# One DRAIN instruction on GpSimd behind the row scatters of the fourth expert tile

## The chip, the core and the metric

The kernel runs on one core of a Trainium2 chip. The core has five engines with queues of their own: TensorE (PE, whose weight loads are shown as PEld), VectorE (DVE), ScalarE (ACT), GpSimd (POOL) and SyncE (SP, which here mostly issues transfers). The metric is the device time of one execution in microseconds; the number compared is the median over several runs.

## What is computed

Three stages follow one another: a chunked state-space scan over 4 x 8 heads, a two-layer network with a leaky ReLU, and a layer of eight experts in which each of the 3072 rows goes through the one expert that its gate picks. The last stage in the reference:

```python
e_idx = np.argmax(logits, axis=1)
gate_w = probs[np.arange(N), e_idx]
out = np.zeros((N, D), dtype=np.float32)
for e in range(E):
    mask = e_idx == e
    h = np.maximum(x[mask] @ w1[e], 0.0)
    out[mask] = gate_w[mask, None] * (h @ w2[e])
```

with N = 3072, D = 256, E = 8 and 1024 hidden columns.

## The kernel before

The scan, the network and the routing are worked off in 128-row chunks and 512-row blocks. For the expert stage the kernel builds, on the chip, a list of row numbers for each expert, and then works through six expert tiles of 512 rows; a seventh and more follow under a condition, which on these inputs is not met.

Three kinds of steps use GpSimd's indirect transfers, in which GpSimd itself makes the descriptors from a list of indices:

- `put` writes 128 row numbers at a time into the experts' lists (L835, tile `il`): 24 transfers.
- `ga` fetches the rows of an expert tile, four transfers of 128 rows each (L977, tile `xg`): 24 for six tiles.
- `sc` scatters 128 finished rows into the output (L1086, `out_dram`): four for each tile, 24 in all.

`oe` on ScalarE (L1082) scales 128 result rows by their gate weight into a buffer, and the `sc` of the same numbers waits for it. `sc.3.3` is the last scatter of the fourth tile (tiles count from 0), `sc.4.0` the first of the fifth.

The order of the instructions on every engine is written out by hand: the string `PLAN` is split into words, each word calls a step, and an engine works its instructions in the order in which the steps wrote them.

```python
for token in PLAN.split():
    fn, *args = token.split(".")
    ...
        STEPS[fn](*args)

u = nc.values_load(tabu, min_val=0, max_val=NFIN, skip_runtime_bounds_check_because=WHY)
```

Behind the last word each engine loads `u`, the number of further tiles (L1197), and branches over their code (L1202). There GpSimd has a few waits and one instruction that the trace calls INC_SWDGE_SEM. What is shown under L1251, the line that opens the program's context, is the end of the program, which the framework adds: every engine has a DRAIN, SP waits for the semaphores of the others, and all meet twice at GpSimd before the program is over. L1238 is its beginning, with a DRAIN on every engine too.

Of the kernel before, what the change touches and what calls it, by code (L numbers as in the profile page):

```python
# [112 lines left out]
    re.3.5 rl.3.5 sl2.4.1 m1.3.6 m2.3.3 re.3.6 rl.3.6 sc.2.1 m1.3.7 sc.2.2 m1.4.0 sh1.5.0 sc.2.3 sh1.5.1 sl1.5.0  # L113
    m2.3.4 re.3.7 sl1.5.1 m2.3.5 re.4.0 rl.3.7 xt.5 rl.4.0 m1.4.1 xe.5.1 xe.5.0 xf.5.1 m2.3.6 re.4.1 xf.5.0 rl.4.1
    m1.4.2 m2.3.7 re.4.2 rl.4.2 m1.4.3 sh2.5.1 sh2.5.0 sl2.5.1 m1.4.4 re.4.3 m2.4.0 oe.3.1 rl.4.3 oe.3.0 oe.3.3
    sl2.5.0 sc.3.0 m1.4.5 oe.3.2 re.4.4 sc.3.1 rl.4.4 m2.4.1 sc.3.2 m2.4.2 re.4.5 rl.4.5 sc.3.3 m1.4.6 m2.4.3 re.4.6
    rl.4.6 m1.4.7 m1.5.0 re.4.7 rl.4.7 m2.4.4 re.5.0 rl.5.0 m1.5.1 m1.5.2 re.5.1 rl.5.1 m2.4.5 re.5.2 rl.5.2 m1.5.3
    m1.5.4 re.5.3 rl.5.3 m2.4.6 re.5.4 rl.5.4 m1.5.5 m1.5.6 re.5.5 rl.5.5 re.5.6 m1.5.7 rl.5.6 m2.4.7 re.5.7 rl.5.7
    oe.4.1 m2q.5.0 oe.4.2 oe.4.0 oe.4.3 sc.4.0 sc.4.1 m2q.5.1 oe.5.0 sc.4.2 sc.4.3 m2q.5.2 oe.5.1 sc.5.0 sc.5.1
# [5 lines left out]
def kernel(  # L125
# [53 lines left out]
    v, s, g, t_ = nc.vector, nc.scalar, nc.gpsimd, nc.tensor  # L179
# [780 lines left out]
    def e_ix(i):  # L960
        tab, k = tl[i]
        vi = nc.values_load(tab[:, 1, k:k + 1], engines=[ENG.SP], min_val=0, max_val=NE * NT - T, skip_runtime_bounds_check_because=WHY)
        gi = sp.tile([P, NQ], I32, tag="gi", name="gi", bufs=6)
        r = nc.sync.dma_start(out=gi, in_=il[bass.ds(vi, T), :].rearrange("(q p) o -> p (q o)", p=P))
        for w in puts:
            tc.add_manual_dep(
                r.ins, w.name, mybir.DependencyInfo(mybir.DependencyClass.Sync, mybir.DependencyReason.DATA),
                reason="the list read here",
            )
        ex.setdefault(i, {})["gi"] = gi  # L970
# [22 lines left out]
    def e_sh(i, t, k):  # L993
        r, hi, lo = e_raw(i, t, k)
        s.copy(out=hi, in_=r)

    def e_sl(i, t, k):
        r, hi, lo = e_raw(i, t, k)
        (g if t == 2 and k == 1 else v).tensor_tensor(out=lo, in0=r, in1=hi.bitcast(F32), op=ALU.subtract)
# [159 lines left out]
    def exp(c, q):  # L1159
# [17 lines left out]
        "tf1": lambda: te.update(fi=table_final()) or next(te["fi"]), "tf2": lambda: next(te["fi"]), "tf3": lambda: next(te["fi"]),  # L1177
        "tf4": lambda: next(te["fi"], None),
        "w1": e_w1, "ixs": lambda: [e_ix(i) for i in range(EARLY, EARLY + NSTAT)], "w2": e_w2, "ix": e_ix, "ga": e_ga, "xt": e_xt, "xe": e_xe, "xf": e_xf, "m1": e_m1, "re": e_re, "rl": e_rl,
        "m2": e_m2, "m2q": e_m2q, "oe": e_oe, "sc": e_sc,  # L1180
        "sh1": lambda i, k: e_sh(i, 1, k), "sl1": lambda i, k: e_sl(i, 1, k),
        "sh2": lambda i, k: e_sh(i, 2, k), "sl2": lambda i, k: e_sl(i, 2, k),
    }
# [72 lines left out]
```

## Time and profile before

| | |
|---|---|
| median of 3 runs | 523.72 us (523.45 to 525.17) |
| the profiled execution's own time | 520.77 us |
| its span, first to last instruction | 519.1 us |
| busy: PE / DVE / ACT / POOL | 494.6 / 328.2 / 288.4 / 137.9 us |
| indirect transfers issued by GpSimd | 72 |
| start of the last one | 507.20 us |

The span is what the trace covers; 1.7 us of the profiled execution's own time lie around it. Busy time of an engine holds no register, branch, semaphore or DRAIN instructions; those stand under the name of the engine's queue, as POOLq or SPq. Times within the span count from its start.

### The profile page before, as it was taken

Reading aid. Unit: us, or ns where it says so; the run is one execution under the profiler, and the core shown is the slowest. Engines: PE = TensorE matmul, PEld = TensorE weight load, DVE = VectorE, ACT = ScalarE, POOL = GpSimd, SP = SyncE. Lnnn points to the kernel's source line nnn. Section 1 sums busy time; section 2 is a strip of 40 time slices with the busy share of each in tenths; the row PEclk is TensorE's granted clock in tenths of the full one; section 3 lists DMA queues with packets and bytes.
Section 4 is the critical chain, followed back from the end, with each engine's and each line's share of the span. In section 5 each row is a group of like instructions: output and inputs, shape, how many; then the busy total and the mean of one; then the engine's idle time right before and its main releaser. Section 6 shows DMA issues by size and latency. Waiting matters only on the chain.

```text
span 519.1 us, 8927 instructions
## 1 busy us (share of the span) xinstructions
PE 494.6 (95%) x3263; PEld 393.6 (76%) x3266; DVE 328.2 (63%) x719; ACT 288.4 (56%) x626; POOL 137.9 (27%) x137
## 2 busy tenths in 40 slices
PE   7879899999999999999999999999999999999990
PEld 4536677787777777777877788888899999899890
DVE  5897999887668664866478777555744544343300
ACT  5858899675475656556564474455525554454220
POOL 5342323040204010121002072300225643715050
PEclk8999999999999999999999999999999999999996
DMA  7988943385713641337000850400018844201010
GB/s 187 171 201 204 277 90 68 62 90 26 161 12 63 113 101 11 61 51 166 0 1 2 259 176 17 40 5 0 2 43 251 289 149 159 70 24 40 1 68 20
DMA packets 120150, 48.41 MB, mean 93 GB/s; under 512 B 84065, under 2 KB 113890, under 8 KB 120098
## 3 DMA queue, kind: packets, MB, share of 16 engines
q1 hardware_dynamic: 117026, 41.35, 36.4%
q0 software_dynamic: 3072, 6.41, 3.8%
q8 instruction: 28, 0.46, 0.5%
q14 instruction: 24, 0.20, 0.2%
HBM read 41.14 MB, written 6.60 MB: 92 GB/s over the span
## 4 chain that ended last, share of the span: by engine, by line
PE 78%; issue 8%; DVE 4%; POOL 3%; ACT 3%; DMA 1%; POOLq 0%; ACTq 0%; DVEq 0%; SPq 0%
PE y L695 24%; PE h L655 24%; PE hp L1025 9%; PE o L1056 9%; PE cb L512 2%; PE psy L552 2%; POOL out_dram L1086 2%; PE psy L547 1%; PE xps L1006 1%; PE yr L852 1%; DMA e<-cumd 1%; DVE hb L605 1%; DVE hb L606 1%; PE lp L734 1%; DVE gg L667 1%
## 5 line engine op out<-in xcount | busy, mean ns | idle before, releaser
L662 ACT ACTIVATE sa<-h 128x512 f32<-128x512 f32 x96 | 56.8, 596 | 72.5 <-PE h L655 71.4
L667 DVE TENSOR_TENSOR gg<-sa,h 128x512 f32<-128x512 f32 x96 | 65.4, 685 | 49.1 <-ACT sa L662 48.9
L677 DVE TENSOR_TENSOR gl<-gg,gh 128x512 fp32r<-128x512 f32 x96 | 71.2, 748 | 14.9 <-ACT gh L672 14.0
L655 PE MATMUL h<-xh,wih 128*128 128x512 f32 x192 | 78.4, 409 | 1.0 <-DVE gg L667 1.0
L695 PE MATMUL y<-gh,woh 128*128 128x512 f32 x192 | 79.2, 412 | 0.0
L695 PE MATMUL y<-gl,woh 128*128 128x512 f32 x192 | 75.4, 393 | 1.4 <-DVE gl L677 1.4
L655 PE MATMUL h<-xl,wih 128*128 128x512 f32 x192 | 75.1, 391 | 0.9 <-DVE xl L576 0.9
L695 PE MATMUL y<-gh,wol 128*128 128x512 f32 x192 | 75.1, 391 | 0.0
L655 PE MATMUL h<-xh,wil 128*128 128x512 f32 x192 | 75.0, 391 | 0.0
L672 ACT CAST gh<-gg 128x512 fp32r<-128x512 f32 x96 | 59.1, 619 | 25.6 <-DVE gg L667 21.2
L1043 DVE SCALAR_TENSOR_TENSOR hl<-hp,hh 128x512 fp32r<-128x512 f32 x48 | 32.9, 689 | 59.5 <-ACT hh L1039 59.2
L1056 PE MATMUL o<-w2s,hh 128*128 128x256 f32 x384 | 70.0, 282 | 0.0
L1025 PE MATMUL hp<-x2h,w1s 128*128 128x512 f32 x192 | 65.5, 394 | 0.1
L1056 PEld LDWEIGHTS o<-w2s,hh 128*128 128x128 f32 x384 | 61.2, 190 | 2.2
L1039 ACT ACTIVATE hh<-hp 128x512 fp32r<-128x512 f32 x48 | 28.6, 598 | 60.8 <-PE hp L1025 58.5
L1056 PE MATMUL o<-w2s,hl 128*128 128x256 f32 x192 | 54.1, 282 | 0.0
L835 POOL DMA_INDIRECT il<-ids,pi x24 | 24.8, 1035 | 105.4 <-DVE base L826 68.2
L417 ACT ACTIVATE e<-e,ncum 128x128 f32<-128x128 f32 x160 | 50.5, 394 | 0.0
L399 POOL TENSOR_SCALAR_AFFINE_SELECT e<-e 128x1024 f32<-128x1024 f32 x20 | 24.2, 1211 | 90.9 <-DMA e<-cumd 84.9
L655 PEld LDWEIGHTS h<-xh,wih 128*128 128x128 f32 x192 | 36.0, 188 | 12.7 <-DVE gg L667 2.9
L695 PEld LDWEIGHTS y<-gh,woh 128*128 128x128 f32 x192 | 36.1, 188 | 11.8 <-issue 4.7
L695 PEld LDWEIGHTS y<-gl,woh 128*128 128x128 f32 x192 | 36.1, 188 | 8.4 <-DVE gl L677 2.3
(209 smaller groups left out, 807.8 us busy)
## 6 DMA issues: line engine op xcount, KB each, us to landing
r<-in_moe_w_dram SPq DMA_DIRECT2D x24, 512.0 KB, 5.3
e<-cumd SPq DMA_DIRECT2D x20, 512.0 KB, 5.2
raw<-in_moe_w_in_dram SPq DMA_DIRECT2D x4, 1024.0 KB, 6.2
raw<-in_moe_w_out_dram SPq DMA_DIRECT2D x4, 1024.0 KB, 6.7
yx<-ysb SPq DMA_DIRECT2D x6, 528.0 KB, 7.4
xt<-in_x_dram SPq DMA_DIRECT2D x24, 128.0 KB, 4.5
ct<-in_C_dram SPq DMA_DIRECT2D x24, 64.0 KB, 4.9
bt<-in_B_dram SPq DMA_DIRECT2D x24, 64.0 KB, 4.2
```

The lines of the kernel that those rows point to most:

```text
L417: s.activation(out=e[:, h, :], in_=i, func=AF.Exp, bias=ncum[:, cc, b * H + h:b * H + h + 1])
L655: t_.matmul(h, lhsT=w[:, k, fs], rhs=xx[:, k, :], start=(i == 0), stop=(i == 5))
L662: s.activation(out=d["sa"], in_=d["h"], func=AF.Copy, scale=0.01)
L667: v.tensor_tensor(out=d["gg"], in0=d["sa"], in1=d["h"], op=ALU.max)
L672: s.copy(out=d["gh"], in_=d["gg"])
L677: v.tensor_tensor(out=gl, in0=d["gg"], in1=d["gh"].bitcast(F32), op=ALU.subtract)
L695: t_.matmul(y_t[j][k], lhsT=w[:, f, ds], rhs=gg, start=(f == 0 and i == 0), stop=(f == NF - 1 and i == 2))
L835: w = g.indirect_dma_start(out=il[:], out_offset=IndirectOffsetOnAxis(ap=pi[:, q:q + 1], axis=0), in_=ids[:, c0 + q:c0 + q + 1], in_offset ...
L1025: t_.matmul(d["hp", f], lhsT=d[1][:, k, part, fs], rhs=xx[:, k, :], start=(n == 0), stop=(n == 5))
L1039: s.activation(out=e_h(i, f, "hh"), in_=ex[i]["hp", f], func=AF.Relu)
L1043: v.scalar_tensor_tensor(out=e_h(i, f, "hl"), in0=d["hp", f], scalar=0.0, in1=d["hh", f].bitcast(F32), op0=ALU.max, op1=ALU.subtract)
L1056: t_.matmul(d["o", q], lhsT=d[h, f][:, q * P:(q + 1) * P], rhs=d[2][:, f, part, :], start=(start and n == 0), stop=(f == NF2 - 1 and n == ...
```

## The change

A word `dr` is added to `PLAN` right behind `sc.3.3`, and the table of steps gets an entry for it that writes a GpSimd DRAIN. Nothing else is added, taken away or moved.

```diff
-    sl2.5.0 sc.3.0 m1.4.5 oe.3.2 re.4.4 sc.3.1 rl.4.4 m2.4.1 sc.3.2 m2.4.2 re.4.5 rl.4.5 sc.3.3 m1.4.6 m2.4.3 re.4.6
+    sl2.5.0 sc.3.0 m1.4.5 oe.3.2 re.4.4 sc.3.1 rl.4.4 m2.4.1 sc.3.2 m2.4.2 re.4.5 rl.4.5 sc.3.3 dr m1.4.6 m2.4.3 re.4.6
...
-        "m2": e_m2, "m2q": e_m2q, "oe": e_oe, "sc": e_sc,
+        "dr": lambda: g.drain(), "m2": e_m2, "m2q": e_m2q, "oe": e_oe, "sc": e_sc,
```

The rows below are GpSimd's order around this place, the change against the kernel before, from the third scatter of the fourth tile to the load of `u`; a name such as `o_5699` is the buffer that the scatter writes out. Register moves, waits and DRAINs are not among the rows of this view.

```order
 L1086 DMA out_dram<-o_5712,gi 3072x256
 L1086 DMA out_dram<-o_5699,gi 3072x256
-L1086 DMA out_dram<-o_5940,gi 3072x256
-L1086 DMA out_dram<-o_5911,gi 3072x256
-L1086 DMA out_dram<-o_5938,gi 3072x256
-L1086 DMA out_dram<-o_5942,gi 3072x256
+L1086 DMA out_dram<-o_5941,gi 3072x256
+L1086 DMA out_dram<-o_5912,gi 3072x256
+L1086 DMA out_dram<-o_5939,gi 3072x256
+L1086 DMA out_dram<-o_5943,gi 3072x256
```

Nothing has moved: from here on the buffers' numbers are one higher, because the DRAIN took a number. It stands between `o_5699` (`sc.3.3`) and `o_5941` (`sc.4.0`), and carries no wait on a semaphore and no post to one. The other engines keep their order.

## Rows read from the trace of the kernel before

**Rows 1.** The page: span, and busy time of each engine.
```profile
span 519.1 us, 8927 instructions
PE 494.6 (95%) x3263; PEld 393.6 (76%) x3266; DVE 328.2 (63%) x719; ACT 288.4 (56%) x626; POOL 137.9 (27%) x137
```
**Rows 2.** Busy time in stretches of the end: us, engines, PE clock, DMA share, GB/s.
```profile
475.00:496.00 21.00, 20.95 (x125) 18.34 (x124) 6.92 (x10) 7.25 (x14) 0.00 (x0) 1.00 0.02 7
...
508.20:509.40 1.20, 0.00 (x0) 0.00 (x0) 0.00 (x0) 0.00 (x0) 0.00 (x0) 1.00 0.33 116
...
512.30:518.20 5.90, 0.00 (x0) 0.00 (x0) 0.00 (x0) 0.00 (x0) 0.00 (x0) 0.50 0.00 0
```
**Rows 3.** Timeline of POOL at the end: start, us, instruction, idle time before it.
```profile
473.92 0.98 POOL L1086 DMA_INDIRECT out_dram<-o,gi  x1 [0.30 <-issue]
496.32 0.98 POOL L1086 DMA_INDIRECT out_dram<-o,gi  x1 [21.41 <-ACT o L1082]
497.60 0.98 POOL L1086 DMA_INDIRECT out_dram<-o,gi  x1 [0.30 <-issue]
...
507.20 0.98 POOL L1086 DMA_INDIRECT out_dram<-o,gi  x1 [1.87 <-ACT o L1082]
```
**Rows 4.** Line 1202, behind the branch: count, ns min/median/max, first and last start.
```profile
L1202 POOLq EVENT_SEMAPHORE  x5: 17/43/43, 510.2 to 510.5; - x5
...
L1202 POOLq INC_SWDGE_SEM  x1: 1628/1628/1628, 510.6 to 510.6; - x1
```
**Rows 5.** Line 1251, the program's end, from 510 to 518.3 us, POOL alone.
```profile
L1251 POOLq DRAIN  x1: 5945/5945/5945, 512.3 to 512.3; - x1
L1251 POOLq EVENT_SEMAPHORE  x1: 17/17/17, 518.3 to 518.3; - x1
```
**Rows 6.** The same line from 512 to 513.5 us, SP alone.
```profile
L1251 SPq EVENT_SEMAPHORE  x12: 27/28/28, 512.2 to 512.9; - x12
L1251 SPq DRAIN  x2: 7/10/13, 512.9 to 513.0; - x2
```
**Rows 7.** Waits of SP's queue, 500 to 521 us: us in total, times, longest.
```profile
SPq L1251 <- DMA out_dram<-o,gi: 68.3, 1, 68.3
SPq L1251 <- PEq L1251: 6.0, 2, 5.4
```
**Rows 8.** Line 1251 from 518.3 us on, POOL alone.
```profile
L1251 POOLq EVENT_SEMAPHORE  x3: 17/17/17, 518.3 to 518.9; - x3
L1251 POOLq DRAIN  x2: 40/74/107, 518.4 to 518.8; - x2
```
**Rows 9.** Line 1238, the program's beginning, POOL alone.
```profile
L1238 POOLq INC_SWDGE_SEM  x1: 27/27/27, 0.2 to 0.2; - x1
...
L1238 POOLq DRAIN  x1: 188/188/188, 0.4 to 0.4; - x1
```
**Rows 10.** DMA issues: count, median us from issue to landing.
```profile
il<-ids,pi POOLq DMA_INDIRECT x24, 9.0
xg<-yx,gi POOLq DMA_INDIRECT x24, 4.1
out_dram<-o,gi POOLq DMA_INDIRECT x24, 2.5
```
**Rows 11.** The last twelve scatters, from 465 us on: durations and landing.
```profile
L1086 POOL DMA_INDIRECT out_dram<-o,gi x12: 977/979/1801, 469.3 to 507.2; - x12
...
DMA to landing us min/median/max: 2.4/2.4/3.2
```
**Rows 12.** The first indirect transfers, line 835, the whole span.
```profile
L835 POOL DMA_INDIRECT il<-ids,pi x24: 975/978/1401, 109.6 to 380.1; - x24
```

## The prediction

> **What bounds the kernel now.** I begin with the page. TensorE is busy for 494.6 of 519.1 us [rows 1], so over most of the span only less work for TensorE would shorten the kernel. The change adds one instruction on GpSimd, which is busy for 137.9 us, so the question is narrow: is GpSimd waited for anywhere near the DRAIN, and does the DRAIN alter anything later?
>
> The busy time in stretches answers the first half. From 475 to 496 us GpSimd does nothing at all, while TensorE is busy for 20.95 of 21 us [rows 2]. The timeline of GpSimd shows the same from its side: `sc.3.3` starts at 473.92 and takes 0.98, so it ends at 474.90, and `sc.4.0` starts at 496.32 because ScalarE's `o` was not there earlier, after 21.41 us of idle time [rows 3]. The DRAIN goes into this gap.
>
> The second half needs the end of the program, where TensorE is done and every microsecond counts fully. The last scatter ends at 507.20 + 0.98 = 508.18 us [rows 3], yet the span lasts to 519.1 [rows 1]: a tail of 10.9 us. I take it apart by the lines behind the branch. GpSimd's waits there start at 510.2, and INC_SWDGE_SEM runs from 510.6 for 1.63 us [rows 4]. Then comes GpSimd's DRAIN at the end of the program: from 512.3, for 5.945 us, up to 518.2 [rows 5]. Behind it 0.84 us of meeting and clearing are left. In the stretch from 512.3 to 518.2 no engine does anything and the DMA share is 0.00 [rows 2]. So more than half of the tail is one DRAIN, alone on the chip, and everybody waits for it: SP is through its own end at 513.0 [rows 6] and then waits 5.4 us, which the view puts down to PE [rows 7], though PE is idle all that time [rows 2].
>
> What does this DRAIN do for 5.9 us? It isn't waiting for work that the profile shows: GpSimd's last instruction ended at 508.18, and the last scatter, issued at 507.20, landed 2.4 to 3.2 us later [rows 3, 11], before the DRAIN began; its data moves from 508.2 to 509.4, with a DMA share of 0.33 [rows 2]. Nor is a DRAIN on GpSimd slow in itself. The same trace has three more: 0.188 us at the beginning of the program, behind nothing but five small instructions [rows 9], and 0.107 and 0.040 us right behind the long one [rows 8]. What sets the long one apart is what lies between it and the previous DRAIN: the whole program, with 24 + 24 + 24 = 72 indirect transfers [rows 10]. Its neighbour tells the same story. INC_SWDGE_SEM took 0.027 us at the beginning [rows 9] and 1.628 us behind the 72 [rows 4]. My reading is that GpSimd keeps something for each indirect transfer it has issued, that nothing cleans it up on the way, and that the DRAIN goes through this list one by one.
>
> **The change part by part.** There is one part, with one cost and one effect.
>
> The cost of the new DRAIN. 64 of the 72 indirect transfers stand ahead of it (24 `put`, 24 `ga`, 16 `sc` of four tiles), 8 behind it (`sc.4.0` to `sc.5.3`). If the long DRAIN is a base of about 0.1 us [rows 8] and a share for each transfer, the share is (5.945 - 0.1) / 72 = 0.081 us. The new DRAIN then takes 0.1 + 64 x 0.081 = 5.3 us. It may first wait for `sc.3.3` to land, at the latest 3.2 us behind its issue [rows 11], at 477.1. So it is over by 482.4. The only thing queued behind it is `sc.4.0`, which ScalarE releases at 496.3; the cover is 21.4 us, 14 us of it to spare. While it lasts nobody waits for GpSimd: the buffers that ScalarE needs back are freed by the landing of the scatters, not by the DRAIN. Without the cover the 5.3 us would delay the eight scatters one for one. I cost it at nothing.
>
> The effect on the last DRAIN. With 8 transfers behind it, it takes 0.1 + 8 x 0.081 = 0.75 us instead of 5.945, 5.2 less.
>
> The effect on INC_SWDGE_SEM is bounded from both sides. At most nothing changes: 1.63 us [rows 4]. At least, if it grows in a straight line from 0.027, it is 0.027 + 8 / 72 x 1.60 = 0.20 us. I take 0.5: it also releases SP (SP's first step of the end passes at 512.2, just as it finishes [rows 6, 4]), so I leave it eight posts at the 0.043 us of a semaphore step [rows 4], 0.34, and scale the other 1.29 by 8 / 72, 0.14. It gains 1.1 us.
>
> What is late next is SP. Its end runs from 512.2 to 513.0 [rows 6], 0.8 us behind INC_SWDGE_SEM. With the old 1.63 us, GpSimd's DRAIN would end at 512.27 + 0.75 = 513.02 and SP arrives at 513.0: a tie, and GpSimd's next step, at 518.26 before [rows 5], comes at 513.07. That is 5.2 us earlier. With 0.5 us both move up by 1.1: 6.3 us earlier. With 0.2 us, 6.6 earlier. So SP doesn't take back what the DRAIN gives, since it hangs on the same INC_SWDGE_SEM.
>
> The sum: 520.77 - 6.3 = **514.5 us** for the profiled execution. The runs shown have a median of 523.72, 2.95 us above that execution. The tail is the same program in both, so I take the 6.3 off the median: **517.4 us**, 1.2% less.
>
> A rule of the Trainium skill speaks against this. PSUM — Partial Sum Buffer, Engine vs sequencer instructions, says that a drain waits for the engine to go fully idle. Read strictly, a DRAIN on an idle engine is short, one written ahead of it changes nothing, and the time would stay at 523.7. This case's trace doesn't agree: the engine's last instruction and the last landing lie ahead of the 5.945 us [rows 3, 5, 11].
>
> **The rivals.** *A fixed toll.* The long DRAIN costs 5.9 us whenever any indirect transfer came before it, be it 8 or 72: fetching a routine, say, or setting up the descriptors anew. Then the new DRAIN takes about 6 us in the gap, the last one 5.9 us again, and the time stays at 523.7. For it: all three short DRAINs have no indirect transfer between them and the DRAIN ahead, so no row tells "some" from "many". Against it: INC_SWDGE_SEM grew as well, and a step of 1.6 us next to one of 5.9 fits a list that both go through better than one routine that is fetched. GPSIMD Engine Reference, in Instruction dispatch, gives about 6 us for the first call into freshly loaded code, with no instruction of its own in the profile; no run here shows yet whether that is what the DRAIN pays.
>
> *A short list.* GpSimd keeps only the last so many transfers. With 16 of them the share is 5.85 / 16 = 0.37 us, and the last DRAIN still takes 0.1 + 8 x 0.37 = 3.0 us, 2.9 less: 520.8. Against it: the transfers' durations show no cleaning up on the way, with 0.98 us at the median from the first to the last [rows 11, 12].
>
> *A slow restart, slower than before.* The DRAIN throws away what GpSimd had prepared, and `sc.4.0` pays to get it back, while the last DRAIN stays at 5.9 us. If the restart costs as much as the long DRAIN, `sc.4.0` ends 6 us late, at 503.3, and the other seven follow at 0.98 + 0.30 = 1.28 us [rows 3]: 503.3 + 9.0 = 512.3 instead of 508.18, so 527.8. The point from which it decides: the last two scatters have some 1.9 us of slack between them, so a restart below 1.9 us is swallowed, and one above shows. Against it: the very first indirect transfer took 1.40 us, only 0.42 more than the median [rows 12].
>
> That the DRAIN isn't where it says is no rival: the order has it between `sc.3.3` and `sc.4.0`. A DRAIN that outlasts the gap would need 21.4 us, four times what the long one took with more behind it.
>
> **How the numbers follow.** Likeliest, 0.82: the list, 517.4, with 517.1 to 518.5 from the bounds on INC_SWDGE_SEM. The short list 0.05, 520.8. The fixed toll 0.09, 523.7. The slow restart 0.04, 527.8. The runs of before spread over 1.7 us, and the profiled execution lies 3 us below their median, so a new median can lie a microsecond or two off the old one; I widen the first case to 515.5 to 520.0, which alone holds about 8 in 10. About 0.3% (1.6 us) is what a measurement of this kernel can tell from no change. Faster takes in the list and the short list, less a little for the spread: 0.86. Same: the toll, 0.09. Slower: 0.05.
>
> **What the profile of the changed kernel would show.** A POOLq DRAIN at about 475 us, of 5 to 8 us; 5 to 6 means no waiting for the landing. `sc.4.0` at 496.3 as before, with its 0.98 us. INC_SWDGE_SEM of 0.2 to 0.6 us; 1.6 would put the gain at 5.2. The last POOLq DRAIN of 0.6 to 0.9 us. SP's end beginning at about 511.1, and a span of 512.5 to 513.9. I am wrong if the last DRAIN is still near 5.9 us (a toll), near 3 (a short list), or if the scatters of the fifth tile begin late.

## The result and the profile after

The changed kernel takes 517.9 us at the median of 4 runs (515.77 to 518.36), the kernel before 524.18 us at the median of 4 runs on the same chip (523.45 to 525.17). The ratio is 0.9871, with a 95% interval of 0.9838 to 0.9904; of 524.18 us that is 5.0 to 8.5 us less. The forecast was 6.3 us less, 517.4 us. The profiled execution took 515.77 us, where 514.5 was forecast.

The page of the changed kernel gives its span and its busy times. The span is 5.0 us shorter, and the busy times are within 1.2 us of those before [rows 1]:

```profile
span 514.1 us, 8931 instructions
PE 495.4 (96%) x3266; PEld 393.5 (77%) x3266; DVE 327.0 (64%) x719; ACT 288.1 (56%) x626; POOL 138.1 (27%) x137
```

The group of the new line, 1180, in the changed kernel: one DRAIN, with its duration in ns and its start in us.

```profile
L1180 POOLq DRAIN  x1: 9710/9710/9710, 471.3 to 471.3; - x1
```

The timeline of POOL in the changed kernel, around that DRAIN and at the end:

```profile
474.75 0.98 POOL L1086 DMA_INDIRECT out_dram<-o,gi  x1 [0.30 <-issue]
497.13 0.98 POOL L1086 DMA_INDIRECT out_dram<-o,gi  x1 [21.41 <-ACT o L1082]
...
508.02 0.98 POOL L1086 DMA_INDIRECT out_dram<-o,gi  x1 [0.48 <-ACT o L1082]
```

The two are read together. The DRAIN's record begins at 471.3, while scatters of the fourth tile are still running, so its 9.71 us hold their time too. What the DRAIN costs is read from its end: 471.3 + 9.71 = 481.0 us. `sc.3.3` ends at 474.75 + 0.98 = 475.73, so the DRAIN holds GpSimd for 5.3 us behind it. `sc.4.0` starts at 497.13, 16 us after the DRAIN is over, and what released it is ScalarE's `o`, after the same 21.41 us of idle time as before [rows 3]. The cover held, and nothing came late because of the DRAIN. In the stretch of the gap TensorE is busy for 21.95 of 22 us, at the full granted clock as before [rows 2]:

```profile
475.00:497.00 22.00, 21.95 (x130) 19.16 (x129) 6.92 (x10) 7.43 (x14) 0.72 (x1) 1.00 0.04 13
```

Now the end. Line 1202 of the changed kernel, behind the branch (count, ns, first and last start), answers to [rows 4]:

```profile
L1202 POOLq EVENT_SEMAPHORE  x5: 17/43/43, 511.7 to 512.0; - x5
L1202 POOLq INC_SWDGE_SEM  x1: 348/348/348, 512.1 to 512.1; - x1
```

Line 1251, the program's end, from 511 to 513.3 us, POOL alone, answers to [rows 5]:

```profile
L1251 POOLq DRAIN  x1: 707/707/707, 512.5 to 512.5; - x1
L1251 POOLq EVENT_SEMAPHORE  x1: 17/17/17, 513.3 to 513.3; - x1
```

The same line from 511 to 513.3 us, SP alone, answers to [rows 6]:

```profile
L1251 SPq EVENT_SEMAPHORE  x12: 27/28/28, 512.4 to 513.1; - x12
L1251 SPq DRAIN  x2: 7/10/13, 513.2 to 513.2; - x2
```

And the waits of SP's queue from 500 us on answer to [rows 7]:

```profile
SPq L1251 <- PEq L1251: 0.7, 2, 0.5
```

The last DRAIN took 0.707 us instead of 5.945, INC_SWDGE_SEM 0.348 instead of 1.628. SP's 6.0 us of waiting for the others became 0.7. GpSimd's DRAIN is over at 512.5 + 0.7 = 513.2, the time at which SP comes through its own steps. So the two tie, and neither gives anything back.

The tail from the end of the last scatter to the end of the span is 514.1 - (508.02 + 0.98) = 5.1 us, against 10.9 us before: 5.8 less in this pair of executions. In experiment e8, a second execution of the same kernel, it is 4.4.

### The profile page after: what moved, and what is told of

Its sections match the earlier page's. It is cut to its first block, busy times and chain, and to the rows that moved or that the text cites. A ratio compares the mean times of both kernels' runs of the same rounds, so it can differ in the third digit from the quotient of the medians.

```text
span 514.1 us, 8931 instructions
## 1 busy us (share of the span) xinstructions
PE 495.4 (96%) x3266; PEld 393.5 (77%) x3266; DVE 327.0 (64%) x719; ACT 288.1 (56%) x626; POOL 138.1 (27%) x137
## 4 chain that ended last, share of the span: by engine, by line
PE 72%; issue 8%; ACT 6%; DVE 5%; POOL 2%; DMA 2%; SPq 2%; POOLq 1%; ACTq 0%; DVEq 0%
PE y L695 22%; PE h L655 22%; PE hp L1025 10%; PE o L1056 9%; PE cb L512 2%; PE psy L552 2%; POOL out_dram L1086 1%; SPq L392 1%; DVE hb L606 1%; PE psy L547 1%; DMA ct<-in_C_dram 1%; PE xps L1006 1%; PE yr L852 1%; DMA e<-cumd 1%; DVE hb L605 1%
## 5 line engine op out<-in xcount | busy, mean ns | idle before, releaser
L1025 PEld LDWEIGHTS hp<-x2h,w1s 128*128 128x128 f32 x192 | 36.1, 188 | 8.3 <-issue 0.9
```

Source lines behind the costliest of these rows:

```text
L1025: t_.matmul(d["hp", f], lhsT=d[1][:, k, part, fs], rhs=xx[:, k, :], start=(n == 0), stop=(n == 5))
```

## The experiments

The theory: GpSimd keeps something for each indirect transfer, a DRAIN goes through what has gathered since the DRAIN ahead of it, and so does INC_SWDGE_SEM. The rivals from before the result, the fixed toll, the short list and the slow restart, had already lost with the 0.707 us. Three were left that can give the same 0.707 us: that the DRAIN goes by the time since the one before it, that it goes by the count of all of GpSimd's instructions, or that the cost hangs on the bytes or rows moved. A further question was where a DRAIN may stand, and whether the gain can be had without the gap. Each kernel is timed against the kernel before on its own chip. In all but e3, e9 and e10 the computation is that of the kernel before, and the word `dr` has the same entry in the table as in the change.

**e1, behind the first tile's scatters.** 44 transfers ahead of the DRAIN, 28 behind.

```diff
-    ... w1.4 m2.1.5 sl1.3.1 xe.2.1 xe.2.0 sc.0.3
+    ... w1.4 m2.1.5 sl1.3.1 xe.2.1 xe.2.0 sc.0.3 dr
```

> The one DRAIN stands behind sc.0.3, in an idle stretch of 10.4 us: 44 indirect transfers ahead of it, 28 behind. The list theory (a base and a share for each transfer since the last DRAIN; from 5.945 us with 72 and 0.707 with 8 the share is 0.082 and the base 0.05): last DRAIN 2.34 us, INC_SWDGE_SEM 0.75 (0.020 for each transfer, 0.19 base), the new DRAIN over 3.7 us after sc.0.3 ends, the time 4.5 us below the kernel before, a ratio of 0.991. Rival, time since the last DRAIN (the same two points give 0.011 us for each us): last DRAIN 1.4 us, time 5.5 us or more below. Rival, all GpSimd instructions since the last DRAIN (140 and 9, now 32): last DRAIN 1.65 us.

519.84 against 524.93 us, ratio 0.9919 (0.9894 to 0.9945). Line 1251 of e1 at the end, POOL alone; the longest of its three DRAINs is the one in question:

```profile
L1251 POOLq DRAIN  x3: 46/107/2341, 514.1 to 517.0; - x3
```

Line 1202 of e1, POOL alone:

```profile
L1202 POOLq INC_SWDGE_SEM  x1: 748/748/748, 513.4 to 513.4; - x1
```

28 transfers behind give 2.341 us and 0.748 us, between the values at 8 and at 72 and on a straight line with them. The rivals of time and of all instructions put other values there and fall, and so does any list with a limit of 28 or less.

One expectation missed. The new DRAIN ends at 419.6, 5.8 us behind `sc.0.3` (412.83 + 1.00 = 413.83), where the share for 44 transfers gives 3.7. The stretch covered it, but the size is off by 2.1 us; what the traces show of it stands beside e6.

**e2, ahead of the first indirect transfer.** None ahead, all 72 behind.

```diff
-    r3.0 yr.0.0 be.0 y.17 yc.0.0 mask.11 gl.18 put.0 yr.0.1
+    r3.0 yr.0.0 be.0 y.17 yc.0.0 mask.11 gl.18 dr put.0 yr.0.1
```

> The one DRAIN stands ahead of the first put: no indirect transfer ahead of it, 72 behind, some 49 other GpSimd instructions ahead. The list theory: the new DRAIN takes about 0.1 us once GpSimd is idle, the last one 5.95 and INC_SWDGE_SEM 1.63 as in the kernel before, the time the same (within 0.3%). Rival, time since the last DRAIN: last DRAIN 4.8 us, 1.2 us less. Rival, all instructions since: last DRAIN about 4.0 us, 1.9 us less.

524.3 against 524.93 us, ratio 0.9987 (0.9964 to 1.0009): no change that can be told. Line 1251 of e2 at the end, POOL alone, shows the full DRAIN of [rows 5] again:

```profile
L1251 POOLq DRAIN  x3: 40/107/5945, 516.6 to 523.1; - x3
```

So a DRAIN somewhere in the program is not enough; indirect transfers must stand ahead of it. This also speaks against a cost that only the first DRAIN of the program pays.

**e5, at the very end.** All 72 ahead, none behind: the DRAIN has no cover at all.

```diff
-    m2q.5.3 oe.5.2 sc.5.2 oe.5.3 sc.5.3
+    m2q.5.3 oe.5.2 sc.5.2 oe.5.3 sc.5.3 dr
```

> The one DRAIN stands behind sc.5.3, the last scatter: all 72 transfers ahead, none behind. The theory that only covered time is saved: the new DRAIN ends 5.95 us after sc.5.3, the load of u, the branch and the fetch behind it start only then; last DRAIN 0.05 to 0.1 us, INC_SWDGE_SEM 0.19; the time 0.8 us above the kernel before (ratio 1.0015), which a measurement can't tell from it. Rival, an early DRAIN saves wherever it stands (or the code behind the branch is fetched while it works): the time 2 us or more below.

522.09 against 521.68 us, ratio 1.0004 (0.9985 to 1.0023). Line 1180 of e5:

```profile
L1180 POOLq DRAIN  x1: 7165/7165/7165, 508.4 to 508.4; - x1
```

Line 1251 of e5 at the end, POOL alone:

```profile
L1251 POOLq DRAIN  x3: 34/41/107, 519.3 to 520.6; - x3
```

The added DRAIN ends at 515.5, that is 5.95 us behind the last scatter (508.58 + 0.98 = 509.56), and the program's own then takes 0.041 us. The same work is done once, at another place, and nothing is won. INC_SWDGE_SEM is shorter here too, 0.189 us, but the load of `u` and the branch, which before ran beside the last scatter, now stand behind the DRAIN. So the change doesn't make the DRAIN's work less: it moves it.

**e4, with too little cover.** 68 ahead, 4 behind; the DRAIN stands between two scatters that TensorE's last work is just releasing.

```diff
-    ... sc.4.2 sc.4.3 m2q.5.2 oe.5.1 sc.5.0 sc.5.1
+    ... sc.4.2 sc.4.3 dr m2q.5.2 oe.5.1 sc.5.0 sc.5.1
```

> The one DRAIN stands behind sc.4.3, where sc.5.0 has its data 0.5 us later: 68 transfers ahead, 4 behind. The theory that its cost counts where no idle time covers it: it holds sc.5.0 until 5.6 us after sc.4.3 ends, so the last scatter starts 3.5 us later than in the kernel before; last DRAIN 0.4 us, INC_SWDGE_SEM 0.27; the time 3.0 us below the kernel before (ratio 0.994), 3.3 above the change. Rival, scatters are made ready and go out while the DRAIN works: last scatter on time, the time 6.5 us below the kernel before.

520.84 against 524.93 us, ratio 0.9929 (0.9908 to 0.9951). Line 1180 of e4:

```profile
L1180 POOLq DRAIN  x1: 9012/9012/9012, 499.9 to 499.9; - x1
```

The timeline of POOL in e4: `sc.4.3`, `sc.5.0` and the last scatter.

```profile
502.32 0.98 POOL L1086 DMA_INDIRECT out_dram<-o,gi  x1 [0.30 <-issue]
509.79 0.98 POOL L1086 DMA_INDIRECT out_dram<-o,gi  x1 [6.49 <-ACT o L1082]
...
513.64 0.98 POOL L1086 DMA_INDIRECT out_dram<-o,gi  x1 [0.30 <-issue]
```

The DRAIN ends at 508.9, 5.63 us behind `sc.4.3`, and `sc.5.0` starts only after it. The view blames ScalarE for the 6.49 us, but the DRAIN lay in the queue for all but the last 0.86 us of them. From the start of `sc.4.0` (498.47) to that of the last scatter it takes 15.17 us, against 10.88 before [rows 3]: 4.3 later, where 3.5 was expected. The tail is 519.0 - 514.62 = 4.4 us, 6.5 shorter. By these parts e4 should gain 2.2 us; it measured 4.1 (2.6 to 4.8 by the interval). The start of `sc.4.0` alone differs by up to 5 us between the profiled executions of these kernels (495.53 in e6, 500.37 in e2), so one execution's parts can't settle the rest. The reading that cover matters stands: the last DRAIN is shorter than in the change (0.381 us), and still about a third of the 6.3 us is gone.

**e6 and e7, a second DRAIN on top of the change**, behind `sc.0.3` and behind `sc.5.1`.

```diff
 e6, beside the change:
-    ... xe.2.1 xe.2.0 sc.0.3
+    ... xe.2.1 xe.2.0 sc.0.3 dr
 e7, beside the change:
-    ... oe.5.1 sc.5.0 sc.5.1
+    ... oe.5.1 sc.5.0 sc.5.1 dr
```

> Two DRAINs, behind sc.0.3 and behind sc.3.3. The theory that a DRAIN empties the list: the second one goes through 20 transfers (64 - 44) and ends 1.7 us after sc.3.3, or when sc.3.3 has landed, some 1.5 to 2.5 us after it, in place of 5.3 with one DRAIN; the last one 0.71 us, INC_SWDGE_SEM 0.35, the time that of the change, ratio 0.987. Rival, a DRAIN goes through all transfers since the beginning: 5.3 us again, and the last one with 8 wouldn't be short.

> The change with a second DRAIN behind sc.5.1, where sc.5.2 has its data 1.9 us later: 6 transfers for it, 2 left for the last one. The list theory: last DRAIN 0.21 us, INC_SWDGE_SEM 0.23; SP's end, 0.8 us behind INC_SWDGE_SEM, now bounds alone, so the tail is 0.1 us shorter at most. The new DRAIN must see sc.5.1 land, some 1.5 to 2 us behind its end, and delays sc.5.2 by 0 to 0.5 us. The time is that of the change within 0.3%. Rival, there is more to get from a shorter last DRAIN: 0.5 us or more below the change.

**e8, the change itself**, run beside these two.

> The change itself once more, beside the runs above: ratio 0.987 to the kernel before, last DRAIN 0.707 us, INC_SWDGE_SEM 0.348, if the numbers depend on the count of transfers alone; a last DRAIN that differs by more than 0.05 us would say that something else is in it.

Against 521.68 us: e6 514.85, ratio 0.9882 (0.9851 to 0.9912); e7 515.65, ratio 0.9898 (0.9869 to 0.9926); e8 515.13, ratio 0.9882 (0.9857 to 0.9907). Neither second DRAIN gains or loses what can be told. Line 1180 of e6, its two DRAINs:

```profile
L1180 POOLq DRAIN  x2: 6680/9162/11645, 404.3 to 469.7; - x2
```

The second one ends at 476.4, 2.3 us behind `sc.3.3` (473.12 + 0.98), where a single one at this place needs 5.3 us: the first had taken its part away. This is the plainest sign that a DRAIN clears what it goes through. By the share alone it would have been 1.7 us for 20 transfers. The other DRAINs written behind a scatter just issued miss the share by more: in e7 the second one ends 2.6 us behind `sc.5.1`, for 6 transfers (0.5 by the share), and the first of e6 ends at 416.0, 5.4 us behind `sc.0.3`, for 44 (3.7 by the share). The scatter `sc.0.3` of e6 in the timeline, and its line with the time to landing:

```profile
409.61 1.00 POOL L1086 DMA_INDIRECT out_dram<-o,gi  x1 [0.31 <-issue]
...
DMA to landing us min/median/max: 4.5/4.5/4.5
```

It lands at 414.1, and the DRAIN ends 1.84 us later. The semaphores in the traces give the landing of the others. Behind it the DRAIN still takes 1.84 us for 44 transfers (e1 too), 0.86 for 20 (e6) and 0.29 for 6 (e7): 0.041 us for each and a base of 0.05, half the share. Where half the share takes longer than the 1.4 us from the scatter's end to its landing, as in the change (half of it is 2.6 us), e4 and e5, the landing adds nothing: the DRAIN takes 5.30 us for 64, 5.63 for 68 and 5.95 for 72 behind the scatter's end. One reading fits all of these: half the share needs no landing, and the other half begins only when the last transfer has landed. It comes from the same runs that it explains, and no run tests it. Line 1251 of e7 at the end, POOL alone:

```profile
L1251 POOLq DRAIN  x3: 46/107/207, 511.9 to 513.2; - x3
```

0.207 us for 2 transfers, half a microsecond less than in the change; yet the tail is 513.5 - 509.0 = 4.5 us, against 4.4 in e8. GpSimd's DRAIN is over at 512.15, and its next step comes at 512.7, when SP is through: SP alone bounds the end there, and shortening GpSimd's side further buys nothing. The second DRAIN also had a price: `sc.5.2` waited for it, and from `sc.4.0` to the last scatter e7 takes 12.26 us, 1.4 more than e8, where 0 to 0.5 was expected. The medians, 0.5 us apart, can't tell that from nothing.

**e3, e9 and e10, more transfers.** The DRAIN of the change is left out. In its place stand 12 (e3, e9) or 6 (e10) extra indirect transfers into a new tile that nobody reads, of 16 rows each (e3, e10) or 128 (e9).

```diff
+    def extra():
+        for k in range(12):
+            w = g.indirect_dma_start(
+                out=il2[:], out_offset=IndirectOffsetOnAxis(ap=ids[0:16, k:k + 1], axis=0),
+                in_=ids[0:16, k:k + 1], in_offset=None, bounds_check=NT - 1, oob_is_err=False,
+            )
...
-    ... re.4.5 rl.4.5 sc.3.3 m1.4.6
+    ... re.4.5 rl.4.5 sc.3.3 xt12 m1.4.6
```

> No added DRAIN. Twelve more indirect transfers of only 16 rows each, into a tile that nobody reads, in the idle stretch behind sc.3.3: 84 transfers in place of 72, 2% more rows. The list theory, a share for each transfer: last DRAIN 6.92 us, INC_SWDGE_SEM 1.87, the time 1.2 us above the kernel before, a ratio of 1.002. Rival, a share for each row or descriptor: last DRAIN 6.07 us. Rival, a short list that is already full at 72: last DRAIN 5.95 us, nothing changes.

> The twelve extra transfers at the same place, with 128 rows each in place of 16, and no added DRAIN. A share for each transfer: last DRAIN 6.92 us and INC_SWDGE_SEM 1.87 as with 16 rows. A share for each row: last DRAIN 6.94 us here, but it was 6.925 with 16 rows, which a share for each row doesn't give. On the 11 us that the run with twelve lost on ScalarE and TensorE between 478 and 500 us: if the 16-row form brought them, sc.4.0 starts near 497 us again and the time is 1.2 us above the kernel before; if twelve transfers in that stretch bring them, 10 us or more above.

> Six extra transfers of 16 rows each at the same place, no added DRAIN: 78 transfers. The list theory: last DRAIN 6.43 us, INC_SWDGE_SEM 1.75. On the 11 us that the run with twelve lost between 478 and 500 us: if each extra transfer brings some of it, about half, the time 5 us above the kernel before; if it was one event that has nothing to do with their count, 11 us or none.

e3: 535.16 against 524.93 us, ratio 1.0222 (1.0172 to 1.0271). e9: 534.9 against 524.18, ratio 1.021 (1.0189 to 1.0231). e10: 526.84 against 524.18, ratio 1.0044 (1.0013 to 1.0075). Line 1261 of e9 and then of e10, the program's end there, POOL alone:

```profile
L1261 POOLq DRAIN  x3: 40/107/6925, 525.5 to 533.0; - x3
```

```profile
L1261 POOLq DRAIN  x3: 40/107/6435, 517.4 to 524.4; - x3
```

The DRAIN grows past 5.945 us as expected: 6.435 us with 78 transfers, 6.925 with 84. It is the same 6.925 in e3, with an eighth of the rows in each extra transfer. So the share goes by transfers and not by rows, and no limit shows up to 84. Nor does it go by bytes: the twelve of e9, of 128 four-byte rows each, add 0.98 us for 6 KB, and the eight scatters of the change take 0.66 above the base for 1 MB.

The whole time missed its expectation widely: e3 and e9 lost 10 to 11 us where the end accounts for 1.2. The loss lies elsewhere. Two stretches of e3, with the columns of [rows 2]:

```profile
485.00:490.00 5.00, 3.42 (x10) 2.86 (x11) 0.69 (x1) 0.60 (x1) 3.18 (x4) 0.67 0.01 0
...
495.00:500.00 5.00, 5.00 (x14) 3.94 (x13) 0.69 (x1) 0.68 (x2) 0.00 (x0) 0.50 0.01 3
```

The waits of ScalarE ahead of `hh` that the view calls `remote`, which means that it names no instruction of this core as what ended them, in e9 from 475 to 500 us (us in total, times, longest), and then in e10:

```profile
ACT hh L1040 <- remote: 10.9, 2, 10.0
```

```profile
ACT hh L1040 <- remote: 3.9, 2, 2.3
```

Around the extra transfers ScalarE stands at its `hh` for 10.9 us in e9 (11.5 in e3, where `sc.4.0` starts only at 508.60), and TensorE runs out of work behind it. The granted clock of e3 falls during that idle time and is still 0.50, the lower of its two levels (1.2 GHz), from 495 to 500 us, where TensorE is busy again for 5.00 of 5 us. In the kernel's order ScalarE's `hh` waits for TensorE's post and not for these transfers. The semaphores in the trace show that the post was late: in e9 the matmul that posts ends at 485.91 and ScalarE starts at 494.77, 0.02 us behind the post; in e8 the posts come 0.01 us behind the end of their matmul. Six extra transfers cost a quarter of what twelve do (2.7 us), and the rows don't matter. Why the posts come late stays open: no run here took the transfers apart from their pace or from their place.

The times of the last DRAIN and of INC_SWDGE_SEM over all runs, by the number of indirect transfers between the last DRAIN written and the program's end:

| transfers behind | kernels | last DRAIN, us | INC_SWDGE_SEM, us |
|---|---|---|---|
| 0 | e5 | 0.041 | 0.189 |
| 2 | e7 | 0.207 | 0.235 |
| 4 | e4 | 0.381 | 0.268 |
| 8 | the change, e8; e6 | 0.707; 0.697 | 0.348 |
| 28 | e1 | 2.341 | 0.748 |
| 72 | before, e2 | 5.945 | 1.628 |
| 78 | e10 | 6.435 | 1.748 |
| 84 | e3, e9 | 6.925 | 1.868 |

The line through 8 and 72 has a share of (5.945 - 0.707) / 64 = 0.082 us for each transfer and a base of 0.05; for INC_SWDGE_SEM (1.628 - 0.348) / 64 = 0.020 and 0.19. At 28, 78 and 84 it gives 2.34, 6.44 and 6.93 us for the DRAIN.

## Why the prediction was right, step by step

**The bound.** That the last DRAIN kept the whole chip waiting was right: with it short, SP's wait at the end fell from 6.0 to 0.7 us, and the span with it.

**The list.** Right in its form: the time of the last DRAIN goes by indirect transfers since the DRAIN ahead (e1, e10, e3), not by rows (e9), and a DRAIN clears what it goes through (e5, e6). That it is a list of something, gone through one by one, remains the reading; the runs show the straight line and the clearing, not the thing itself. The rule named ahead, from the Trainium skill's PSUM — Partial Sum Buffer, Engine vs sequencer instructions, that a drain waits until the engine is idle, isn't wrong here (the new DRAIN did wait for the scatters ahead of it) but leaves out the 5.9 us. The fixed toll falls too: with it, 8 transfers could not have come at 0.707 us and 28 at 2.341. The Trainium skill's GPSIMD Engine Reference, Instruction dispatch, gives about 6 us for the first call into freshly loaded code; these values speak against that as what the DRAIN pays.

**The cost of the new DRAIN.** Forecast 5.3 us, or up to 7.5 with a wait for the landing ahead of it, measured 5.3 behind `sc.3.3`, with 16 us of the cover left (14 forecast). The exact fit hangs on the early landing: the same sum is 2.1 us short in e1. So "5 to 6 means no waiting for the landing" was wrong as a sign: a DRAIN doesn't end before the landing (e1, e6, e7), but here the landing fell inside the 5.3 us. Its record was misjudged, "at about 475 us, of 5 to 8 us": it starts at 471.3 and is 9.71 long, since it begins while the scatters ahead still run. No term of the sum hangs on either. "I cost it at nothing" was right, and e4 shows what it costs without the gap.

**The effect on the last DRAIN.** Forecast 0.75, measured 0.707; the base was 0.05 rather than 0.1.

**INC_SWDGE_SEM.** Forecast between 0.20 and 1.63, taken at 0.5, measured 0.348. The eight posts that I kept for SP were not in it in that size: its fixed part is 0.19 us. The gain is 1.28 instead of 1.1.

**SP as the next one late.** Right: GpSimd's DRAIN is over and SP comes through at the same 513.2, and in e7, with a still shorter DRAIN, GpSimd waits 0.5 us for SP.

**The sum.** The two terms give 5.24 + 1.28 = 6.5 us. The profiled pair shows 5.8 less in the tail, since the stretch from the end of the last scatter to the first wait behind the branch was 2.7 us (509.0 to 511.7), against 2.0 before (508.18 to 510.2 [rows 3, 4]). This stretch varies with or without the DRAIN: 2.0 us in e8 (508.97 to 511.0), 2.3 in e2 (512.24 to 514.5). The profiled execution was also 0.8 us later already at the fourth tile's scatters, ahead of the new DRAIN. Together they account for a span of 514.1 where 512.5 to 513.9 was forecast, and for SP's end at 512.4 instead of 511.1. The medians, 6.28 us apart here and 6.55 in e8, lie close to the 6.3; with intervals of some 3 us, so close a fit is in part luck.

## What to carry to other kernels

Where GpSimd has issued many indirect transfers, look at the last DRAIN of the program: here it cost 0.05 us and 0.082 us more for each transfer since the DRAIN ahead, with the chip idle beside it. A plain DRAIN in a late gap of GpSimd moves that time under other work; ask of the gap that it is longer than the DRAIN (0.082 us for each transfer ahead, and more where the last transfer lands late: 5.8 us instead of 3.7 in e1) and that few transfers stand behind it. At the very end it moves nothing, and in a gap too short it delays what is queued behind it.

## What the runs showed of the hardware that was not expected

INC_SWDGE_SEM grows with the same count, 0.020 us for each transfer, on a fixed 0.19, and a DRAIN written late makes it shorter too. The record of a DRAIN on GpSimd starts while instructions ahead of it still run, so its length is no cost: 9.71 us in the record, 5.3 behind the last scatter. A DRAIN right behind a transfer doesn't end before that transfer has landed, and behind a late landing it still took half the share, 0.041 us for each transfer (e1, e6, e7). And twelve small indirect transfers in a row, which nothing waited for, came with a post of TensorE 8.8 us late and held up ScalarE for 10.9 us; the kernel lost some 9 us beyond the longer end, for a reason that stays open.
